# Moving a few weight-preparing steps, and one set of hash products, inside a fused attention and feed-forward kernel

## The chip, the cores and the metric

The kernel runs on one core of one Trainium2 chip. The metric is the time of one execution on the device in microseconds (us), the median of three runs. The profile is one further execution, taken by the hardware profiler; its span starts at the first instruction.

A core has five instruction streams that run side by side and wait for one another by semaphores: PE (matrix products; its weight loads are shown as PEld), DVE (vector operations), ACT (activations, copies and scalings), POOL and SP (here mostly issuers of transfers). Products are written to PSUM, and a product can only be written where an earlier one has been read out.

## The reference

Attention with hashed buckets, and a gated feed-forward block behind it:

```python
# q, k, v: (4 batches, 8 heads, 768 positions, 64); proj: (64, 6)
q_bits = einsum('bhsd,dk->bhsk', q, proj) > 0        # 6 bits make a bucket
k_bits = einsum('bhsd,dk->bhsk', k, proj) > 0
mask = q_bucket[:, :, :, None] == k_bucket[:, :, None, :]
scores = where(mask, q @ k^T / sqrt(64), -1e9)
attn = softmax(scores)
x = (attn @ v)  ->  (3072 tokens, 512)

g = x @ w_gate                                       # (512, 1536)
out = (g * sigmoid(g) * (x @ w_val)) @ w_out         # (1536, 512)
```

The three weight matrices arrive as float64 and are used as float32.

## The kernel before

Heads are taken in pairs, so there are 16 pairs: 0 to 3 are batch one, 4 to 7 batch two, and so on. Each pair has two halves of the queries (384 each), and each half has six score units, one for every 128 keys. The unit number `u` counts through them, so half h of pair n begins at `u = 12 n + 6 h`. `LATE = 48` is the start of batch two and `MOVE = 84` that of pair 7.

While batch one is attended, nothing is known yet for the feed-forward block, and the weights are made ready meanwhile: converted from float64 words in 36 pieces, and, for gate and value, combined into the sums that Strassen's scheme needs. This is written as one generator of small steps. A piece takes three VectorE operations (lines 302, 304 and 307), after ScalarE has scaled it (288, 289); a block of four pieces is followed by four forming operations (336); at the end come 12 operations on the down weights (359).

```python
    def narrow(i):
        ...
        scale_to(i + 1)
        nc.vector.tensor_single_scalar(wi, wi, 3, op=ALU.logical_shift_left)       # 302
        yield True
        nc.vector.scalar_tensor_tensor(out=wi, in0=hi, ...)                        # 304
        yield True
        nc.vector.tensor_tensor(wi, wi, lo, op=ALU.add)                            # 307
        progress["piece"] = i + 1
        load_words(i)            # asks for the next pieces, on POOL's queue
        yield True

    def prepare():
        for n in range(2 * DF // PIECE):          # six blocks
            for j in range(NJ):                   # of four pieces
                yield from narrow(n * NJ + j)
            yield from form(n)                    # four steps, then written out to DRAM
            progress["blocks"] = n + 1
        for f in range(NF):                       # twelve pieces of w_out
            yield from narrow(2 * NJ * DF // PIECE + f)
        ...                                       # twelve steps on them (359)

    def prepare_on(n):
        for _ in range(n):
            next(preparing, None)

    def scale_ahead():
        scale_to(min(progress["piece"] + 4, progress["scaled"] + 1))
```

PSUM has one tile for attend, shared in batch one with the sum of a pair's exponentials, and seven that go round for all else:

```python
    av_ps = ctx.enter_context(tc.tile_pool(name="av_ps", bufs=1, space=PSUM))
    banks = ctx.enter_context(tc.tile_pool(name="ps", bufs=7, space=PSUM))
    ...
    def total(n):
        ps = av_ps.tile([P, 512], FP32, tag="av", name="sum") if b == 0 else bank("sum")
        ...                                       # products with a column of ones (531)
        nc.vector.reciprocal(r, ps[:, 0:HQ])      # 539
        ...                                       # eight transfers by SP (544), then norm (551)
```

The next pair's hash bits come from four small products and are spread to a second set of rows by a transfer on SP's queue. Before pair 4, that queue also fetches q and k of pair 5 in eight transfers of small pieces (104).

```python
        def hash_early(todo):
            q0, q1, *ks = hash_blocks(todo)       # four products into one PSUM tile
            q0()                                  # signs of q, on ScalarE
            q1()
            spread_q()                            # SP: qb rows 64.. <- qb rows 0.. (420)
            return [...]                          # signs of k, done after the half's scores
```

The main loop takes one half after the other:

```python
    for u in range(0, N, NCH):
        n, half, _ = units[u]
        gating = u >= LATE
        ...
        for c in range(NCH):
            score(u + c)
            if u + c == 2 or not gating and half == 1 and c == NCH - 3:
                prepare_pair(1)                   # the next pair's hash products
            if c == 1 and half == 0 and 0 < n <= NP:
                total(n - 1)
            if c:
                add(u + c)
        ...
        for c in range(NCH):
            attend(u + c)
        ...
        prepare_on(0 if u == LATE else 4)
        ...
        prepare_on(0 if LATE - NCH <= u <= LATE else 3)
        if not gating:
            continue
        ...
        while atoms and (credit > 0 or not end):  # 14 up steps of the feed-forward block
            size, atom, end = atoms.pop(0)
            credit -= size
            atom()
            part += size
            ...
            if 5 < part < 14 if u == LATE else part < 9:
                prepare_on(size)
            if 6 < part < 11 or u == LATE and part > 10:
                scale_ahead()
            ...
```

From batch two on, every half carries 14 steps of the feed-forward block of the batch before: up steps (product, then copies, additions, tanh and gate on ScalarE and VectorE), or down steps. The first down product is due in the first half of pair 7, and what is then left of the preparing is done ahead of it.

Of the kernel before, what the change touches and what calls it, by code (L numbers as in the profile page):

```python
# [18 lines left out]
def kernel(  # L19
# [16 lines left out]
    NCH = S // P  # L36
# [72 lines left out]
    def load(n, names):  # L109
        if n < len(pairs):  # L110
            for name in names:
                fetch(n, name, nc.sync)
# [179 lines left out]
    def scale_ahead():  # L292
        scale_to(min(progress["piece"] + 4, progress["scaled"] + 1))
# [70 lines left out]
# [3 lines that stand above are left out]
# [102 lines left out]
    LATE = NP * 2 * NCH  # L469
# [5 lines left out]
    def score(u):  # L475
        n, half, c = units[u]
        qs = slice(half * HQ, (half + 1) * HQ)
        ks = slice(c * P, (c + 1) * P)
        sc = [bank("sc")[:, 0:HQ] for _ in range(2)]
        for x, start in ((T, True), (bits, False)):  # L480
            if u < 2 and not start:
                prepare_pair(1)
            for h in range(2):
                rows = slice(h * D, (h + 1) * D)
                nc.tensor.matmul(sc[h], x["k", n][rows, ks], x["q", n][rows, qs],  # L485
                                 start=start, stop=not start)
        for h in range(2):
            nc.scalar.activation(weights(u)[:, h, 0:HQ], sc[h], AF.Exp,  # L488
                                 scale=SCALE * (OFF / 2 if n <= NP else 1.0))

    def attend(u):
        n, half, c = units[u]
        b, pr = pairs[n]
        a = weights(u)
        if c == 0:
            av[n] = av_ps.tile([P, 512], FP32, tag="av", name="av")
        ps = av[n]
        width = AW if half == 0 else HQ
        for h in range(2):
            nc.tensor.matmul(ps[h * D : (h + 1) * D, 0:width], raws["v", n][:, h, c, :],  # L500
                             a[:, h, 0:width], start=c == 0, stop=c == NCH - 1)
        if c == NCH - 1:
            if half == 0:
                xT[b, pr] = xp.tile([P, S], FP32, tag="xT", name="xT")
                mean[n] = att.tile([P, 1], FP32, tag="e", name="e")
                nc.scalar.activation(mean[n], ps[:, HQ : HQ + 1], AF.Copy, scale=EPS)
            nc.scalar.copy(xT[b, pr][:, half * HQ : (half + 1) * HQ], ps[:, 0:HQ])

    def add(u):
        n, half, c = units[u]  # L510
        a = weights(u)
        if c == 1:
            acc[n, half] = att.tile([P, 2, HQ], FP32, tag="acc", name="acc")
            nc.vector.scalar_tensor_tensor(out=acc[n, half], in0=weights(u - 1)[:, :, 0:HQ],
                                           scalar=S * EPS / P, in1=a[:, :, 0:HQ],
                                           op0=ALU.add, op1=ALU.add)
        elif c > 1:
            nc.vector.tensor_tensor(acc[n, half], acc[n, half], a[:, :, 0:HQ], op=ALU.add)  # L518

    def total(n):  # L520

        b, pr = pairs[n]

        ps = av_ps.tile([P, 512], FP32, tag="av", name="sum") if b == 0 else bank("sum")
        t = [acc.pop((n, half)) for half in range(2)]
        for h in range(2):
            for half in range(2):
                g = (2 * h + half) * BLOCK  # L530
                nc.tensor.matmul(ps[g : g + BLOCK, 0:HQ], ones, t[half][:, h, :],  # L531
                                 start=True, stop=True)
        if b == 0:
            space = wo.rearrange("p f m -> p (f m)")
            space = space[:, n % 2 * 3 * HQ : (n % 2 + 1) * 3 * HQ].rearrange("p (x q) -> p x q", q=HQ)
            r, t = space[:, 2, :], space[:, 0:2, :]
        else:
            r, t = t[1][:, 0, :], t[0]
        nc.vector.reciprocal(r, ps[:, 0:HQ])  # L539
        for half in range(2):  # L540
            for h in range(2):
                g = (2 * h + half) * BLOCK
                for at in (h * D, h * D + BLOCK):
                    nc.sync.dma_start(t[at : at + BLOCK, half, :], r[g : g + BLOCK, :])
        waiting.append(lambda: norm(n, t))
        if pr == NP - 1:
            push_ffn(b)
# [200 lines left out]
    def prepare_pair(count):  # L748
        for _ in range(count):
            rest.extend(f for f in steps.pop(0)() or [] if f)  # L750

    def finish(todo):
        while todo:
            todo.pop(0)()
# [5 lines left out]
# [3 lines that stand above are left out]
        if u == MOVE:  # L763
            progress["late"] = True
            for t in late_ring:
                nc.gpsimd.memset(t[:, :, HQ:AW], 1.0)
        for c in range(NCH):
            score(u + c)
            if u + c == 2 or not gating and half == 1 and c == NCH - 3:
                prepare_pair(1)  # L770
            if c == 1 and half == 0 and 0 < n <= NP:
                total(n - 1)
            if c:
                add(u + c)
        if n <= NP:
            finish(waiting)
            finish(rest)
        if not gating and half == 0:
            steps = front(n + 1)
        if not gating and half == 0 and u > 0:  # L780
            prepare_pair(2)
        for _ in range(1 if u else 2):
# [5 lines that stand above are left out]
        if half == 1:  # L788
            load(n + 2, "qkv" if gating else "v")
        elif not gating:  # L790
            prepare_pair(2 if u > 0 else 4)
            load(n + 2, "qk")
        finish(first)
        prepare_on(0 if u == LATE else 4)
        chores = []
        if half == 1 and n >= NP:
            total(n)
            if n + 1 < len(pairs):
                chores = [None] + steps.pop(0)()
        prepare_on(0 if LATE - NCH <= u <= LATE else 3)  # L800
        if not gating:
            continue
        if n + 1 < len(pairs) and half == 0:
            steps = front(n + 1)
            chores = [None, steps.pop(0), None, steps.pop(0)]

        credit += 14 if n < 2 * NP else 15.75
        end = True
        part = 0
        while atoms and (credit > 0 or not end):  # L810
# [4 lines that stand above are left out]
            if part >= 11 or u + NCH == N and part >= 6:  # L815
                finish(waiting)
                if u + NCH == N:
                    finish([first.pop(0) for _ in range(min(2, len(first)))])
            if 5 < part < 14 if u == LATE else part < 9:
                prepare_on(size)  # L820
            if 6 < part < 11 or u == LATE and part > 10:
                scale_ahead()
            for _ in range(size):
                if chores:
                    step = chores.pop(0)
                    chores.extend(step and step() or [])
        while chores:
            step = chores.pop(0)
            chores.extend(step and step() or [])
# [34 lines left out]
```

## Time and profile before

| | |
|---|---|
| time, median of three runs | 1001.18 us (1000.87 to 1002.05) |
| span of the profiled execution | 1000.3 us |
| VectorE and ScalarE busy over the whole span | 57% and 40% |
| the same in the first 300 us | 82% and 61% |
| one preparing step on VectorE | 0.4 to 0.7 us |
| reciprocal of a sum | 2.55 us |
| six score units on PE, without a break | 5.05 us |
| attend of one half | 4.0 us |
| 14 up steps | 18.26 us |

The kernel has four batches of the same attention work, but batch one also has the preparing and no feed-forward work beside it, and batch two still has preparing steps between its up steps. The shares of the whole span are therefore averages over stages with different limits, and the change lies in the first 280 us only. In the profile, a line of the timeline gives start, duration, engine, line of the kernel, operation, output and inputs; what is in square brackets is the idle time of the engine just before, and what ended it.

### The profile page before, as it was taken

The numbers are of one execution on the slowest core, as the hardware profiler recorded it, in microseconds if no ns is written. First come the engines' busy times: TensorE is split into PE (matmuls) and PEld (weight loads), VectorE is DVE, ScalarE is ACT, GpSimd is POOL, SyncE is SP. The second block draws the span as 40 slices with busy tenths as digits, with TensorE's granted clock in tenths as the row PEclk, the third lists the DMA queues.
The fourth block names the chain that finished last, engine by engine and source line by source line (L and its number), as shares of the span: only waits on it lengthen the run. The fifth ranks groups of instructions, "written<-read, shape, count | busy, mean of one in ns | idle before, by whom it ended". The sixth has DMA issues, their size and how long they took to land.

```text
span 1000.3 us, 12465 instructions
## 1 busy us (share of the span) xinstructions
PE 990.2 (99%) x4597; PEld 599.8 (60%) x4597; DVE 570.7 (57%) x892; ACT 398.4 (40%) x885; POOL 101.5 (10%) x200
## 2 busy tenths in 40 slices
PE   9999999999999999999999999999999999999998
PEld 4444455555576765555557775555556786555687
DVE  5888998887873624556564443554556442435431
ACT  6988555465323214444342223334343211222200
POOL 3222022221000000000000000000000000111000
PEclk9999999999999999999999999999999999999999
DMA  7777595885213032333331204333122012323001
GB/s 230 214 252 244 146 259 161 216 291 148 76 43 76 22 96 84 87 100 95 97 103 34 69 17 116 92 90 100 44 84 77 22 38 64 105 82 111 29 27 37
DMA packets 120749, 106.95 MB, mean 107 GB/s; under 512 B 89264, under 2 KB 104080, under 8 KB 120688
## 3 DMA queue, kind: packets, MB, share of 16 engines
q0 software_dynamic: 19104, 73.28, 22.9%
q1 hardware_dynamic: 100784, 32.67, 14.3%
q8 instruction: 36, 0.59, 0.3%
q10 hardware_dynamic: 800, 0.20, 0.1%
q14 instruction: 25, 0.20, 0.1%
HBM read 81.79 MB, written 17.30 MB: 99 GB/s over the span
## 4 chain that ended last, share of the span: by engine, by line
PE 87%; DMA 2%; DVE 1%; SPq 1%; ACT 1%; issue 1%; POOL 0%; DVEq 0%; POOLq 0%
PE up L575 43%; PE po L575 22%; PE sc L485 12%; PE av L500 9%; PE sum L531 1%; DMA words<-in_moe_w_out_dram 1%; PE hps L403 1%; SPq L104 1%; DMA wo<-wo 1%; DMA qb<-qb 0%; DMA room<-ram 0%; DVE room L359 0%; ACT A L488 0%; DVE wo L539 0%; DVE acc L518 0%
## 5 line engine op out<-in xcount | busy, mean ns | idle before, releaser
L575 PE MATMUL up<-xT,room 128*128 128x384 f32 x768 | 260.9, 488 | 0.0
L575 PEld LDWEIGHTS up<-xT,room 128*128 128x128 f32 x768 | 144.6, 190 | 106.7 <-issue 9.8
L575 PE MATMUL up<-xc,room 128*128 128x384 f32 x576 | 197.4, 486 | 0.0
L485 PE MATMUL sc<-qT,kT 64*128 64x384 f32 x768 | 161.5, 494 | 0.2 <-DVE c L562 0.2
L575 PEld LDWEIGHTS up<-xc,room 128*128 128x128 f32 x576 | 109.5, 190 | 76.3
L579 DVE TENSOR_TENSOR c<-c,up 128x384 f32<-128x384 f32 x72 | 39.8, 553 | 180.1 <-PE up L575 179.7
L518 DVE TENSOR_TENSOR acc<-acc,A 128x768 f32<-128x768 f32 x128 | 122.7, 958 | 14.4 <-ACT A L488 1.0
L318 POOL DMA_DIRECT2D room<-ram x96 | 52.4, 546 | 714.3 <-PE up L575 707.2
L488 ACT ACTIVATE A<-sc 128x384 f32<-128x384 f32 x256 | 105.6, 499 | 3.5 <-PE sc L485 3.4
L485 PEld LDWEIGHTS sc<-qT,kT 64*128 64x128 f32 x768 | 67.8, 186 | 55.5 <-issue 45.7
L710 ACT COPY o<-po 128x256 f32<-128x256 f32 x48 | 17.9, 372 | 200.5 <-PE po L575 200.5
L561 ACT ACTIVATE th<-c 128x384 f32<-128x384 f32 x72 | 37.6, 522 | 128.7 <-DVE c L562 89.2
L500 PE MATMUL av<-A,vraw 128*64 128x384 f32 (+1 forms) x512 | 88.2, 486 | 0.0
L579 DVE TENSOR_TENSOR o<-o,po 128x256 f32<-128x256 f32 x36 | 15.2, 421 | 111.6 <-PE po L575 82.5
L485 PE MATMUL sc<-qb,kb 64*128 64x384 bf16 x384 | 65.4, 323 | 1.7 <-DMA qb<-qb 1.2
L488 ACT ACTIVATE room<-sc 128x384 f32<-128x384 f32 x128 | 54.0, 495 | 32.6 <-PE sc L485 32.6
L575 PE MATMUL po<-wo,hid 128*128 128x256 f32 x288 | 66.9, 382 | 0.0
L575 PE MATMUL po<-wo,room 128*128 128x256 f32 x288 | 66.3, 379 | 0.1
L575 PE MATMUL po<-room,hid 128*128 128x256 f32 x288 | 66.1, 379 | 0.0
L500 PEld LDWEIGHTS av<-A,vraw 128*64 128x64 f32 x512 | 36.7, 137 | 46.0 <-issue 44.1
L638 ACT COPY c<-up 128x384 f32<-128x384 f32 x72 | 34.4, 478 | 69.1 <-PE up L575 69.1
L575 PEld LDWEIGHTS po<-wo,hid 128*128 128x128 f32 x288 | 54.1, 190 | 12.1 <-issue 4.9
(110 smaller groups left out, 969.4 us busy)
## 6 DMA issues: line engine op xcount, KB each, us to landing
room<-ram POOLq DMA_DIRECT2D x48, 512.0 KB, 4.8
room<-ram POOLq DMA_DIRECT2D x48, 384.0 KB, 3.9
vraw<-in_v_dram SPq DMA_DIRECT2D x16, 384.0 KB, 3.3
ram<-room POOLq DMA_DIRECT2D x12, 512.0 KB, 4.8
out_dram<-o SPq DMA_DIRECT2D x48, 128.0 KB, 1.7
room<-in_moe_w_out_dram POOLq DMA_DIRECT2D x10, 512.0 KB, 6.3
qraw<-in_q_dram SPq DMA_DIRECT2D x48, 96.0 KB, 3.2
hid<-in_moe_w_gate_dram POOLq DMA_DIRECT2D x9, 512.0 KB, 6.9
```

The lines of the kernel that those rows point to most:

```text
L104: queue.dma_start(blocks[at : at + BLOCK], src[b, 2 * pr + h][:, x * BLOCK : (x + 1) * BLOCK].rearrange("(a p c) d -> p c a d", c=NCH, p=B ...
L318: nc.gpsimd.dma_start(places[k % 2][:, PARTS[go], :], ram[k % NG][:, PARTS[go], :])
L403: nc.tensor.matmul(tile_[i * BLOCK : (i + 1) * BLOCK, 0:HQ], hash_w, T[name, n][:, half * HQ : (half + 1) * HQ], start=True, stop=True)
L485: nc.tensor.matmul(sc[h], x["k", n][rows, ks], x["q", n][rows, qs], start=start, stop=not start)
L488: nc.scalar.activation(weights(u)[:, h, 0:HQ], sc[h], AF.Exp, scale=SCALE * (OFF / 2 if n <= NP else 1.0))
L500: nc.tensor.matmul(ps[h * D : (h + 1) * D, 0:width], raws["v", n][:, h, c, :], a[:, h, 0:width], start=c == 0, stop=c == NCH - 1)
L518: nc.vector.tensor_tensor(acc[n, half], acc[n, half], a[:, :, 0:HQ], op=ALU.add)
L561: nc.scalar.activation(th, g, AF.Tanh, scale=0.5)
L575: nc.tensor.matmul(ps, a, x, start=start and i == 0, stop=i == len(pairs_) - 1, skip_group_check=True)
L579: nc.vector.tensor_tensor(o, a, b, op=op)
L638: nc.scalar.copy(tile_of(g, spot), c)
L710: nc.scalar.copy(o, c)
```

## The change

Three conditions are changed. The second halves of batch one's pairs 0 to 2 call two preparing steps fewer. From unit 66 on, which is the second half of pair 5, the halves that have up steps call preparing steps behind ten of these and no longer behind eight. And the next pair's hash products are put behind the third score unit of the half before it, not behind the fourth. The purpose is to relieve VectorE in batch one, where it has the sums of the exponentials, the reciprocals and the preparing to do at once, and to have the hash bits earlier; no operation is added or taken out.

```diff
         for c in range(NCH):
             score(u + c)
-            if u + c == 2 or not gating and half == 1 and c == NCH - 3:
+            if u + c == 2 or not gating and half == 1 and c == 2:
                 prepare_pair(1)
@@
-        prepare_on(0 if LATE - NCH <= u <= LATE else 3)
+        prepare_on(0 if LATE - NCH <= u <= LATE else 3 if gating or not half else 1)
         if not gating:
             continue
@@
-            if 5 < part < 14 if u == LATE else part < 9:
+            if 5 < part < 14 if u == LATE else part < (9 if u < LATE + 3 * NCH else 11):
                 prepare_on(size)
```

## The prediction

> **What bounds the kernel now.** I read the page first: part 1 for the shares, part 2 for where they are not even, then the chain that ended last, the waits of PE, stretches cut at the scores of each half pair, and the order of DVE, ACT, SP and PE around each break.
>
> ```profile
> PE 990.2 (99%) x4597; PEld 599.8 (60%) x4597; DVE 570.7 (57%) x892; ACT 398.4 (40%) x885; POOL 101.5 (10%) x200
> ```
>
> PE bounds the span, so only a moment in which PE stands or crawls can be gained. The stretches (us, then busy us of PE, PEld, DVE, ACT, POOL) show where these lie in batch one, pairs 2 to 4, one stretch from the first scores of a half to those of the next:
>
> ```profile
> 53.45:67.63 14.18, 12.46 (x82) 5.83 (x80) 13.32 (x16) 10.25 (x25) 4.80 (x8) 1.00 0.94 344
> 67.63:77.68 10.05, 10.05 (x69) 4.42 (x68) 7.42 (x12) 9.92 (x22) 0.58 (x1) 1.00 0.58 154
> 77.68:92.12 14.44, 12.65 (x83) 5.84 (x81) 13.68 (x16) 10.34 (x25) 3.71 (x7) 1.00 0.85 292
> 102.17:113.79 11.62, 10.45 (x71) 4.53 (x69) 10.92 (x13) 8.04 (x18) 0.53 (x1) 1.00 0.70 215
> ```
>
> A first half without a break would take 5.05 (scores) + 0.78 (sum) + 4.04 (attend), all from the chain, + twice 0.8 (transposes): about 11.5. Pairs 2 and 3 lose 2.7 and 2.9 us there. What PE waited for, and the order on DVE and PE:
>
> ```profile
> PE av L500 <- DVE wo L539: 3.0, 2, 1.7
> PE sc L485 <- DMA qb<-qb: 1.2, 1, 1.2
> ```
> ```profile
> 58.75 0.69 DVE L304 SCALAR_TENSOR_TENSOR room<-hid,room 128x512 int32<-128x512 int32 x1
> 59.57 0.69 DVE L307 CUSTOM_DVE_ANT_0 room<-hid,room 128x1024 uint16<-128x1024 uint16 x1
> 60.18 2.55 DVE L539 RECIPROCAL wo<-sum 128x384 f32<-128x384 f32 x1
> ...
> 84.67 2.55 DVE L539 RECIPROCAL wo<-sum 128x384 f32<-128x384 f32 x1
> ```
> ```profile
> 62.79 1.52 PE L500 MATMUL av<-room,vraw 128*64 128x386 f32 x8 [1.67 <-DVE wo L539]
> ...
> 80.81 0.85 PE L531 MATMUL sum<-acc,ones 128*32 128x384 f32 x6 [0.35 <-DVE acc L518]
> ...
> 87.27 1.52 PE L500 MATMUL av<-room,vraw 128*64 128x386 f32 x8 [1.38 <-DVE wo L539]
> ```
>
> The sum and attend share one PSUM tile, so attend waits for the reciprocal that reads the sum. The reciprocal stands on DVE right behind the preparing steps of the second half before it: the sum ended by 56.9, the reciprocal began at 60.18.
>
> Later, in batch two, PE is dense, but two score stages are longer than 5.05: 216.82 to 222.94 (6.12) and 245.24 to 251.28 (6.04). There ACT stands behind a weight that has not landed, tanh comes late, and DVE frees a bank late:
>
> ```profile
> 216.18 0.67 ACT L288 ACTIVATE wo<-words 128x512 f32<-128x512 f32 x1 [1.77 <-DMA words<-in_moe_w_out_dram]
> ...
> 244.45 0.67 ACT L288 ACTIVATE wo<-room 128x512 f32<-128x512 f32 x1 [2.79 <-DMA room<-in_moe_w_out_dram]
> ```
> ```profile
> 246.11 0.56 DVE L562 SCALAR_TENSOR_TENSOR c<-th,c 128x384 f32<-128x384 f32 x1 [2.32 <-ACT th L561]
> ...
> 266.06 0.56 DVE L579 TENSOR_TENSOR c<-c,up 128x384 f32<-128x384 f32 x1 [2.01 <-PE up L575]
> ...
> 276.42 0.55 DVE L562 SCALAR_TENSOR_TENSOR c<-c,up 128x384 f32<-128x384 f32 x1
> ```
>
> From 266.06 to 292 DVE has no idle gap, and the second down product begins behind it (chain: DVE to 288.24, PE from 288.29).
>
> [...] a ready reciprocal stands 3.3 us behind steps that nobody is waiting for. [...] the kernel uses seven in rotation and one for attend, and the trace shows scores waiting for a bank that DVE's last gate holds. [...] the 48 KB spread of q's bits lands after 4.77 us behind eight small-piece fetches, against a median of 1.9.
>
> **The change part by part.** (1) Fewer steps. A block has 4 x 3 narrowing and 4 forming steps, about 0.61 us each (seven took 55.90 to 60.18). The second halves of pairs 0, 1, 2 call 5 instead of 7; pair 3's had 4 and keeps them. By the start of batch two 47 steps are done, not 53.
>
> Pair 0's cut lets the first reciprocal start when its sum ends, near 34.45 instead of 35.67; PE did not wait there. The normalising and all behind it shift by about 1.2, less 0.3 because other kinds of steps fall into the next half: pair 1's sums are ready by about 55.15, not 55.93. The sum products then take 0.8 instead of 1.4: -0.6. Then five steps (302, 304, 307, 302, 304: 2.95) instead of seven (4.28): the reciprocal ends near 60.65 instead of 62.73. PE is ready for attend at 60.45: it starts at 60.7 instead of 62.79, **-2.1** in all.
> In pair 3 the sum still waits, since its sums come through normalising and its transfers, which shift with the reciprocal (18 us from reciprocal to sum, 16.8 on PE). Five steps again (a forming one, 302, 304, 307, 302: 2.94) instead of seven (4.08): **-1.1** on the second wait. Together **-3.2** by about 91 us.
>
> (2) The hash products move one unit (0.8 us) earlier. The spread before pair 4 does not move for it:
>
> ```profile
> 92.46 2.75 SPq L104 DMA_DIRECT2D qraw<-in_q_dram  x4
> 95.25 3.83 SPq L104 DMA_DIRECT2D kraw<-in_k_dram  x4
> 99.59 0.55 SPq L420 DMA_DIRECT2D qb<-qb  x1
> ```
>
> q's signs end at 97.85 on ACT, and SP gets to the spread at 99.59, behind eight fetches. So the 1.2 us wait for qb stays, whole. In the other pairs it was ready anyway. The price: the products' bank now comes round for the first score of the next half, not its second unit, and the signs of k that read it end there within 0.2 us of PE (53.56 against 53.45). **+0.1**.
>
> (3) The six steps come back in the three halves from 188 us on, two each, behind up steps nine and ten. Counts after each half of batch two: before 61, 76, 91, 106, 121, 136; after 55, 70, 85, 102, 119, 136. No product has to pull a block forward (block 5 of the weights is due at 65 calls with 69 done, the ninth at 97 with 99).
> - First half with two more (188 on): DVE has 1.77 + 0.27 of idle there for 1.3 us of steps. The weight ACT scales last is again one that was asked for three up steps before: **+0.2**.
> - Second (217 on): the fourth scaling after the sixth step now takes a piece whose load is issued one up step later (1.3 us), behind another 512 KB. It lands about 1.0 later, and tanh, gate and bank with it: **+1.0**.
> - Third (245 on): two steps more in the stretch where DVE has no gap, 2 x 0.61: **+1.2**, at the scores or at the down product, not at both.
>
> Sum: -3.2 + 0.1 + 0.2 + 1.0 + 1.2 = -0.7; with a little slack in the later terms I take -0.9: 1001.18 - 0.9 = 1000.3.
>
> **The rivals.** The late steps are absorbed: DVE is idle for 2.3 us waiting for tanh in the second half, and if that gap moves to the third, and the load lands no later, nearly all of -3.2 stays: 998.1. Against it: DVE's gapless 22 us before the down product.
> The later loads collide: the forming of the last block and its 1.8 MB now fall at 203 to 209, beside the fetch of the next weights, and the piece asked for at 208.7 comes 2 us later than I think; then scores at 217 lose as much: 1002.3. For it: that fetch took 7.5 us already. Against it: before, 2 MB moved in the same microseconds.
> The hash move is the gain: if SP's last fetch at 95.25 (3.83 us for four, against 2.75) waited for something that comes earlier now, the qb wait of 1.2 could go: another -0.8. Nothing in the waits of SP says so.
>
> **Range and chances.** The gain is sure to about 0.4, the cost lies between 0.3 and 3.5. 80%: 998.5 to 1001.9. All of it is under 0.4% of the time; 2% would be 20 us, more than all waits of PE.
>
> **What would show it.** Right: attend of pair 2 starts near 60.7 and of pair 3 near 84.1, with gaps under 0.5; the sum of pair 3 still breaks off; the qb wait is still 1.2 at about 101; the up stage starts near 110.6 instead of 113.79; then PE gives back about 1 us near 245 and 1.2 between 272 and 288. Wrong: an up stage that starts later than 112, or a lead of 3 us that is still there at 300, or one that is gone at 220.

## Result, and the profile after

The changed kernel takes **1007.11 us**, the median of four runs (1006.69 to 1008.13); the kernel before takes 1001.62 beside it (1000.87 to 1002.75). The ratio is **1.0055**, 95% interval 1.0038 to 1.0073. Predicted were 1000.3 and a range of 998.5 to 1001.9: the change makes the kernel slower, by some 5.5 us, and the range missed it. The profiled executions differ by 4.4 us (spans 1004.7 and 1000.3).

The page of the changed kernel, part 1, in the same order of engines as before:

```profile
PE 993.3 (99%) x4597; PEld 601.0 (60%) x4597; DVE 570.0 (57%) x892; ACT 399.9 (40%) x885; POOL 101.2 (10%) x200
```

PE is busy 3.1 us longer with the same 4597 products (993.3 against 990.2): part of it ran at a lower clock (0.80 on average from 100.44 to 117.76). The stretches, cut as before at the first scores of each half (pair 2's halves, pair 3's first half, and pair 4's first half; us, then busy us of PE, PEld, DVE, ACT, POOL, granted clock, share of the DMA engines, GB/s), show where:

```profile
53.44:66.61 13.17, 12.61 (x82) 5.79 (x80) 12.44 (x14) 10.34 (x25) 3.41 (x7) 1.00 0.93 319
66.61:76.68 10.07, 10.07 (x71) 4.44 (x70) 6.89 (x11) 9.48 (x21) 2.95 (x4) 1.00 0.59 147
76.68:90.40 13.72, 12.57 (x84) 5.82 (x82) 12.92 (x15) 10.11 (x24) 3.23 (x6) 1.00 0.58 184
...
100.44:117.76 17.32, 13.33 (x70) 5.46 (x68) 16.12 (x19) 9.05 (x19) 3.50 (x6) 0.80 0.61 164
```

Pair 2's first half is 1.0 us shorter than before (13.17 against 14.18) and pair 3's 0.7 (13.72 against 14.44). Pair 4's first half, which had 11.62, has 17.32, with a mean clock of 0.80. It begins 1.7 us earlier than before, at 100.44 instead of 102.17, and its up stage starts 4.0 us later, at 117.76 instead of 113.72. From there on the delay hardly changes: 4.1 at 216.8 of the kernel before, 3.5 at 245.2, 4.2 at the first down product (288.27 against 284.03). So nearly all of the loss in this execution arises within one half pair.

PE's waits (us in total, times, longest), and its order of work around them:

```profile
PE sc L485 <- DMA qb<-qb: 4.0, 1, 4.0
...
PE sum L531 <- DVE acc L518: 1.3, 2, 1.0
...
PE av L500 <- DVE wo L539: 0.2, 1, 0.2
```
```profile
61.77 1.52 PE L500 MATMUL av<-room,vraw 128*64 128x386 f32 x8 [0.24 <-DVE wo L539]
...
80.35 0.85 PE L531 MATMUL sum<-acc,ones 128*32 128x384 f32 x6 [1.04 <-DVE acc L518]
...
105.50 0.47 PE L485 MATMUL sc<-qb,kb 64*128 64x384 bf16 x1 [3.99 <-DMA qb<-qb]
```

The wait of attend for the reciprocal, 3.0 us in two places before, is gone but for 0.2. In its place the wait for q's bits before pair 4 has grown from 1.2 to 4.0. VectorE and SP in the stretch before it, first two lines of the kernel before, then the changed one:

```profile
93.74 1.02 DVE L551 SCALAR_TENSOR_TENSOR xT<-xT,e,wo 128x768 f32<-128x768 f32 x1 [1.46 <-DMA wo<-wo]
```
```profile
87.24 5.04 SPq L544 DMA_DIRECT2D wo<-wo  x8
```
```profile
82.94 2.55 DVE L539 RECIPROCAL wo<-sum 128x384 f32<-128x384 f32 x1
...
97.03 1.02 DVE L551 SCALAR_TENSOR_TENSOR xT<-xT,e,wo 128x768 f32<-128x768 f32 x1 [6.48 <-DMA qraw<-in_q_dram]
```
```profile
85.52 6.80 SPq L544 DMA_DIRECT2D wo<-wo  x8
92.42 3.91 SPq L104 DMA_DIRECT2D qraw<-in_q_dram  x4
96.36 3.94 SPq L104 DMA_DIRECT2D kraw<-in_k_dram  x4
100.83 0.55 SPq L420 DMA_DIRECT2D qb<-qb  x1
```

The reciprocal comes 1.7 us earlier than before (82.94 against 84.67), but normalising comes 3.3 us later: at 97.03, against 93.74 before, where VectorE had been idle for 1.46 us instead of 6.48. SP's issues are slower as well (6.80 us for the eight transfers `wo<-wo`, against 5.04): the spread is issued at 100.83 instead of 99.59.

### The profile page after: what moved, and what is told of

It is laid out like the page before. It is cut to its first block, busy times and chain, and to the rows that moved or that the text cites. A ratio compares the mean times of both kernels' runs of the same rounds, so it can differ in the third digit from the quotient of the medians.

```text
span 1004.7 us, 12470 instructions
## 1 busy us (share of the span) xinstructions
PE 993.3 (99%) x4597; PEld 601.0 (60%) x4597; DVE 570.0 (57%) x892; ACT 399.9 (40%) x885; POOL 101.2 (10%) x200
## 4 chain that ended last, share of the span: by engine, by line
PE 74%; issue 2%; DVE 1%; DMA 1%; ACT 0%; POOL 0%; POOLq 0%; DVEq 0%
PE up L575 34%; PE po L575 21%; PE sc L485 9%; PE av L500 7%; PE sum L531 1%; DMA room<-in_moe_w_out_dram 1%; PE hps L403 1%; DVE room L359 0%; DVE acc L518 0%; ACT A L488 0%; DVE wo L359 0%; DVE c L562 0%; POOL room L318 0%; ACT wo L288 0%; ACT room L289 0%
## 5 line engine op out<-in xcount | busy, mean ns | idle before, releaser
L485 PE MATMUL sc<-qT,kT 64*128 64x384 f32 x768 | 163.7, 500 | 0.2 <-DVE c L562 0.2
```

## What moved in front of SP's transfers

The steps that were cut also trigger transfers. Behind a block's fourth forming step its sums are written out, in two transfers of 512 KB; for blocks 0 and 1 a set is also loaded back (`bring`), behind the write that it reads; and a narrowed piece asks for the next. The cuts in pairs 0 and 1, four steps together, move the end of block 1 from the first to the second half of pair 2. POOL's issues, of the kernel before and then of the changed one:

```profile
74.14 0.58 POOL L339 DMA_DIRECT2D ram<-room  x1 [10.63 <-DVE room L336]
78.26 1.09 POOL L318 DMA_DIRECT2D room<-ram  x2 [3.55 <-issue]
```
```profile
81.19 0.58 POOL L339 DMA_DIRECT2D ram<-room  x1 [4.83 <-DVE room L336]
84.66 1.09 POOL L318 DMA_DIRECT2D room<-ram  x2 [2.89 <-issue]
85.74 0.54 POOL L339 DMA_DIRECT2D ram<-room  x1
86.27 0.53 POOL L273 DMA_DIRECT2D words<-in_moe_w_val_dram  x1
86.78 0.53 POOL L273 DMA_DIRECT2D hid<-in_moe_w_val_dram  x1
```

The load of block 1's set (512 and 384 KB), a write of sums and two pieces of 512 KB now start at 84.7 to 87.3 us, together with the eight small transfers of the reciprocal (85.52 on). Two stretches of six microseconds, before and after, same columns as above:

```profile
84.00:90.00 6.00, 4.62 (x34) 2.34 (x32) 5.79 (x6) 3.88 (x9) 0.53 (x1) 1.00 1.02 413
90.00:96.00 6.00, 6.00 (x48) 2.92 (x44) 4.30 (x6) 4.55 (x13) 0.00 (x0) 1.00 0.59 123
```
```profile
84.00:90.00 6.00, 5.89 (x40) 2.77 (x37) 5.58 (x6) 3.71 (x10) 2.65 (x5) 1.00 0.66 189
90.00:96.00 6.00, 6.00 (x47) 3.01 (x47) 0.55 (x1) 5.51 (x14) 0.00 (x0) 1.00 1.09 319
```

Before, most of the bulk (413 GB/s) is over when the eight transfers (from 87.24 on) and the fetch of q and k need the engines (123 GB/s, 59% busy). After, it is the other way round: the engines are full from 90 to 96, and VectorE works 0.55 us of the six. The transfers issued from 84 to 108 us (count, KB each, median us from issue to landing), before and then after:

```profile
wo<-wo SPq DMA_DIRECT2D x8, 48.0 KB, 3.6
qraw<-in_q_dram SPq DMA_DIRECT2D x4, 96.0 KB, 3.0
```
```profile
wo<-wo SPq DMA_DIRECT2D x8, 48.0 KB, 6.0
qraw<-in_q_dram SPq DMA_DIRECT2D x4, 96.0 KB, 4.5
```

That is a correlation between two executions. The experiments below ask whether it is the cause.

## The experiments

Every ratio is to the kernel before, run on the same chip; brackets hold the 95% interval. Lines of code are those of the changed kernel unless it says otherwise. In one table, with the start of the first up stage of the profiled execution (113.7 before, 117.8 changed):

| run | time, us | ratio | up stage starts |
|---|---|---|---|
| e1: cut steps, hash products back | 1007.54 | 1.0051 [1.0038, 1.0064] | 116.6 |
| e2: hash products alone | 1002.21 | 0.9997 [0.9988, 1.0006] | 112.6 |
| e3: changed, pair 5's q and k later | 1007.74 | 1.0049 [1.0035, 1.0063] | 117.8 |
| e4: changed, PE kept busy in the wait | 1007.61 | 1.0059 [1.0041, 1.0078] | 117.0 |
| e5: cut in pairs 1 and 2 only | 1013.17 | 1.0099 [1.0079, 1.0119] | 111.9 |
| e6: e5 and e3 together | 1011.42 | 1.0097 [1.0081, 1.0112] | 111.8 |
| e7: before, pair 5's q and k later | 1006.09 | 1.0039 [1.0026, 1.0053] | 113.5 |
| e8: before, with bulk added | 1005.94 | 1.0045 [1.0031, 1.0059] | 117.4 |
| e9: e5, look-ahead 3 | 1000.02 | 0.9974 [0.9964, 0.9983] | 112.2 |
| e10: before, look-ahead 3 | 1000.62 | 0.9988 [0.9982, 0.9995] | 113.4 |
| e11: changed, look-ahead 3 | 1005.41 | 1.0030 [1.0019, 1.0041] | 116.2 |
| e12: changed, nothing made up | 1011.00 | 1.0084 [1.0070, 1.0098] | 117.4 |
| e13: changed, block 1's load later | 1005.68 | 1.0035 [1.0020, 1.0049] | 115.1 |
| e14: e13, look-ahead 3 | 1003.83 | 1.0014 [1.0005, 1.0023] | 115.0 |

**Which part does it: e1 and e2.** e1 keeps the cut and the making-up and puts the hash products back; e2 does the reverse on the kernel before.

```diff
-            if u + c == 2 or not gating and half == 1 and c == 2:
+            if u + c == 2 or not gating and half == 1 and c == NCH - 3:
```

> The changed kernel with the hash products back behind the fourth score unit; the steps stay as changed. Traffic theory (the cut of steps moves block 1's forming and loads from 74-85 us to 81-93 us, onto SP's transfers for pair 3's sum and pair 5's q and k, so the spread before pair 4 is issued and lands late, PE stands 4 us and then runs at half clock for 6 us): as slow as the changed kernel, 1006 to 1008, with the wait for qb still near 4 us. Hash theory (the earlier products crowd ScalarE and PE and the spread suffers from it): back near 1001 or lower, wait for qb near 1.

> The kernel before with only the hash products moved behind the third score unit; all preparing steps as before. Traffic theory: 1001 to 1002, the wait for qb stays between 0.8 and 1.5 us, since the spread stands behind SP's fetches. Hash theory: 1005 to 1008.

e1 loses as much as the whole change, e2 nothing: the moved steps carry all of it, and what the hash products cost or bring is too small to see (under 1 us). In e2's profile the wait for q's bits is gone, against what was expected, and the up stage starts 1.1 us earlier than before, yet the median of the time is the same. In e1 VectorE again idles 6.1 us before normalising (97.07). Its wait for q's bits is only 2.5 us, but waits for sums (1.1) and for the reciprocal (0.85) follow it in pair 4: the delay is split in another way.

**Two waits side by side: e3 and e4.** e3 takes the fetch of pair 5's q and k out of SP's way: it goes behind pair 4's first half, where v is fetched. e4 leaves the waits and puts 16 small products that nobody reads ahead of the waiting one, so that PE doesn't stand.

```diff
-            load(n + 2, "qkv" if gating else "v")
+            load(n + 2, "qkv" if n >= NP - 1 else "v")
@@
-            load(n + 2, "qk")
+            load(n + 2 if n < NP - 1 else len(pairs), "qk")
```
```diff
+            if u == LATE and not start:
+                fill = bank("fill")
+                for _ in range(16):
+                    nc.tensor.matmul(fill, sides["k", 1][:, 0:P], sides["k", 1][:, 0:512],
+                                     start=True, stop=True)
```

> The changed kernel, but pair 5's q and k are fetched after the second half of pair 3 has been attended and not after its first half: the spread no longer stands behind these eight fetches. Traffic theory: the wait for qb goes (under 0.3 us) and with it the half clock: 1007.1 - 4.0 - 2.9 = about 1000, and lower if the bulk transfers around 90 us are done by then. Hash theory: 1005 or more, for the place of the products is unchanged. It could lose some of it again if the fetches, now near 100 us, delay the transfers for pair 3's normalising and with them the up stage.

> The changed kernel with 16 bf16 products of 512 columns, whose result nobody reads, put ahead of the product that waits for qb: about 3.4 us of work in the 4 us gap. If the half clock comes from PE's standing still: granted clock 1.0 from 101 to 114 us and 1007.1 - 2.9 = about 1004.2, with the qb wait itself unchanged (what is idle shrinks to under 1 us, the product still starts near 105.5). If the half clock has another cause (the stage or the load of the chip): clock 0.5 again after 104 us and 1007 or a little more.

Both are misses. In e3 the spread is issued at 95.20, and the wait for it is gone. The up stage starts at 117.8 all the same, because another wait takes its place; first VectorE, then PE's longest wait in e3:

```profile
96.48 1.02 DVE L551 SCALAR_TENSOR_TENSOR xT<-xT,e,wo 128x768 f32<-128x768 f32 x1 [5.85 <-DMA wo<-wo]
```
```profile
106.86 1.50 PE L531 MATMUL sum<-acc,ones 128*32 128x384 f32 x6 [3.69 <-DVE acc L518]
```

Normalising is late with no fetch of q and k ahead of it, so the fetch isn't what holds it up, although the profile of the changed kernel names q's fetch beside it. And pair 3's second sums, which VectorE makes behind normalising, come about as late as the spread (in the changed kernel they end at 107.3, and PE has the spread bits at 105.5). In e4 the clock stays at 1.0 from 102 to 112 us, and the up stage still starts only 0.8 us earlier: waits for sums and reciprocal (0.7 and 0.85) show up instead. The halved clock had cost PE some 3 us in the changed kernel (3.1 of busy time), but most of that lay beside VectorE's delay.

**Cutting elsewhere: e5 and e6.** Here pair 0 keeps its two steps, and only pairs 1 and 2 are cut; block 1 then ends in pair 2's first half, as in the kernel before. e6 adds e3's move.

```diff
-        prepare_on(0 if LATE - NCH <= u <= LATE else 3 if gating or not half else 1)
+        prepare_on(0 if LATE - NCH <= u <= LATE else 3 if gating or not half or n == 0 else 1)
```

> The changed kernel, but pair 0's second half keeps its seven steps: four steps fewer before batch two and not six, and block 1 of the weights is formed, written and loaded in the first half of pair 2 as in the kernel before (near 74 to 80 us). Traffic theory: pair 2's normalising no longer waits 6 us (it comes near 92 to 93 us), PE's waits before pair 4 are 1.5 us or less and the up stage starts near 111 to 112; the time is 999 to 1002, depending on what the later halves give back. Rival (too few steps are done before batch two, wherever their transfers lie): 1004 or more.

> As the kernel with four steps fewer, and pair 5's q and k fetched after pair 3's second half. If SP's order is what is left of the wait before pair 4: 1 us lower than that kernel, 998 to 1001, and the wait for qb gone. If the transfers for the normalising set the pace there anyway: the same as that kernel.

In batch one, e5 is what the prediction had hoped for: block 1's load is issued at 79.58, normalising comes at 92.64 (idle 2.2), the wait for q's bits is 1.0, and the up stage starts at 111.9, 5.9 us earlier than in the changed kernel and 1.8 earlier than before. Yet the time is the longest of all, 1013.17 (its profile is of the shortest of its six runs, 1008.04). It loses in batch two, where PE waits 2.2, 1.75 and 0.84 us at three score stages for banks that VectorE's gate holds (L562), behind ScalarE:

```profile
187.82 0.67 ACT L288 ACTIVATE wo<-room 128x512 f32<-128x512 f32 x1 [4.19 <-DMA room<-in_moe_w_out_dram]
...
219.22 0.67 ACT L288 ACTIVATE wo<-room 128x512 f32<-128x512 f32 x1 [2.56 <-DMA room<-in_moe_w_out_dram]
```

By counting, the last piece that ScalarE scales in the halves from `u` = 60, 66 and 72 was asked for three, two and one up steps earlier in e5; in the changed kernel three, three and two. In e5 ScalarE stood 4.19 us at a weight still on its way (187.82 above) and did the tanh only behind it, at 188.95; VectorE's gate, at 189.49, had waited 4.50 us for that tanh. e6 gains no more in batch one: its wait for q's bits is replaced by 1.25 for sums and 0.6 for the reciprocal, as e3 would have it; its time, 1011.42, misses as well.

**The suspect alone, added: e7 and e8.** Both change the kernel before. e7 moves the fetch of q and k as in e3. e8 leaves every step where it is and loads the sets of blocks 0 and 1 once more, four transfers with 1.8 MB in all, ahead of the eight small transfers of pair 2's reciprocal (from 82.72 us on; the changed kernel loads 0.9 MB from 84.66 on, with a write and two pieces behind):

```diff
+        if u == 6 * NCH:
+            for x in range(2):
+                for go in range(2):
+                    bring(x, go)
```

> The kernel before with only that fetch moved: the wait for qb (1.2 us) goes, 1000 to 1001. If it comes back as a wait for the sum or for the reciprocal, or at the scores of batch two: 1001.5 to 1002.5.

> The kernel before, with the first two sets of block sums (1.8 MB) loaded a second time, from about 85.5 us on: nothing else is changed, and no step moves. Traffic theory: the eight transfers behind pair 2's reciprocal land 3 to 4 us later, its normalising comes at 96 to 98 us and not at 93.7, PE waits 2.5 us or more before pair 4's scores or sum, and the time is 1003.5 to 1006. Rival (what is slow in the changed kernel is the order of the steps on VectorE, not the transfers): 1001 to 1002.5.

e7 is slower, against what was expected: the wait for q's bits goes, but the fetch now runs beside the transfers of the last sum, and PE stands 2.1 us in the up stage for the last normalising (117.94). So moving the fetch gains nothing in the kernel before either. e8, with its VectorE steps untouched, becomes the changed kernel in batch one; its VectorE, and its two stretches:

```profile
97.78 1.02 DVE L551 SCALAR_TENSOR_TENSOR xT<-xT,e,wo 128x768 f32<-128x768 f32 x1 [6.48 <-DMA qraw<-in_q_dram]
```
```profile
84.00:90.00 6.00, 4.64 (x32) 2.27 (x30) 5.69 (x5) 2.93 (x7) 1.49 (x3) 1.00 1.04 425
90.00:96.00 6.00, 6.00 (x46) 2.97 (x44) 1.21 (x2) 5.52 (x15) 0.00 (x0) 1.00 1.03 327
```

The same 6.48 us of idle VectorE, a wait of 3.4 us for q's bits, an up stage from 117.35. Bulk at this place is enough to produce the loss of batch one.

**The suspect alone, taken away: e13 and e14.** e13 is the changed kernel, with its steps where they are and one difference: the load of block 1's set, 0.9 MB, waits until the start of batch two, where it still stands ahead of the first up steps. e14 shortens ScalarE's look-ahead on top.

```diff
                 for go in range(2):
-                    bring(i, go)
+                    if i == 0:
+                        bring(i, go)
@@
+        if u == LATE:
+            bring(1, 0)
+            bring(1, 1)
         if n <= NP:
```

> Theory (bulk transfers that now fall behind pair 2's second half hold up the small ones of SP): block 1's share of them, the load of one set of the gate and value weights, two transfers of 0.9 MB together, leaves 84 to 86 us and is asked for at the start of batch two, the steps on VectorE staying where the change puts them. About 0.9 of some 3 MB are gone from 81 to 88 us, so the normalising of pair 3 comes at 94.5 to 96 instead of 97.0, its idle time before it falls from 6.5 to 3 to 5, and the up stage starts 1 to 3 earlier than 117.8. Time 1003.5 to 1006.5. Rival 1 (the steps themselves, in their new order on VectorE, make normalising late): normalising stays at 97 and the time at 1007. Rival 2 (the load only moves the collision on, to the spread at 101): normalising earlier, but the wait for qb before pair 4 stays at 3 or more, and the time at 1006.5 to 1008.

> The same with the look-ahead of ScalarE shortened from four to three pieces. Theory (two independent losses): the shorter look-ahead takes about 2 off, as it did for the changed kernel alone, so 1001.5 to 1004.5, and the late score stages are 5.05 where they were 5.5 to 6.1. Rival (the loss in batch one and the late one are one and the same): less than 1 us between the two.

VectorE, SP and POOL of e13 (whose line numbers behind 341 are one higher), and its small transfers issued from 84 to 108 us:

```profile
91.99 1.02 DVE L552 SCALAR_TENSOR_TENSOR xT<-xT,e,wo 128x768 f32<-128x768 f32 x1 [1.40 <-DMA wo<-wo]
```
```profile
85.55 4.99 SPq L545 DMA_DIRECT2D wo<-wo  x8
90.64 2.75 SPq L104 DMA_DIRECT2D qraw<-in_q_dram  x4
93.43 3.53 SPq L104 DMA_DIRECT2D kraw<-in_k_dram  x4
97.48 0.55 SPq L421 DMA_DIRECT2D qb<-qb  x1
```
```profile
81.16 1.12 POOL L339 DMA_DIRECT2D ram<-room  x2 [4.82 <-DVE room L336]
82.28 0.53 POOL L273 DMA_DIRECT2D words<-in_moe_w_val_dram  x1
83.22 0.53 POOL L273 DMA_DIRECT2D hid<-in_moe_w_val_dram  x1 [0.41 <-ACT A L489]
```
```profile
wo<-wo SPq DMA_DIRECT2D x8, 48.0 KB, 3.3
...
qb<-qb SPq DMA_DIRECT2D x1, 48.0 KB, 6.6
```

More has changed place than the 0.9 MB. In the changed kernel POOL issued the load at 84.66, after 2.89 us without an issue, and the second write of sums and the two pieces, 0.5 MB each, right behind it; without the load these are issued 3.6 to 4.0 us earlier. With all this bulk out of the way, the eight small transfers land after 3.3 us again, and normalising comes at 91.99, 5.0 us earlier than in the changed kernel and 1.75 earlier than before: the shift that the prediction had counted on. Of the second rival a part is true: the spread, although issued 3.4 us earlier than in the changed kernel, lands after 6.6 us, perhaps because two weight pieces of 512 KB are asked for at 94.88 and 96.67, just ahead of it. They too have been moved by the cut (83.17 and 84.96 before). So PE still waits 2.6 us for q's bits, runs at half clock for 3.4 us, and starts the up stage at 115.1: 2.7 us of the 4.0 are back. The time falls by less, 1.4 us, and by medians of different chips (ratios 1.0055 and 1.0035, whose intervals overlap), so that the gain in time is less sure than the one in the trace; in e13's profile a wait of 1.1 us at 249.9 takes some of it.

**The loss in batch two: e9, e10, e11, e14.** One digit, in four kernels: ScalarE may scale three pieces ahead of VectorE and no longer four.

```diff
-        scale_to(min(progress["piece"] + 4, progress["scaled"] + 1))
+        scale_to(min(progress["piece"] + 3, progress["scaled"] + 1))
```

> The kernel with four steps fewer (pair 0 uncut), and ScalarE allowed to scale three pieces ahead of VectorE instead of four, so that it never stands behind a piece that was asked for one to three up steps before. Look-ahead theory (the later losses, 2.2, 1.75 and 0.84 us at the scores at 186, 218 and 250 us of that kernel, come from ScalarE standing behind such a piece): those three waits go, the up stage still starts near 112, and the time is 998.5 to 1001.5, some of the gain being lost where VectorE now has to wait for a scaling. Rival (the later losses come from VectorE having too many steps left): 1007 or more, as without it.

> The kernel before with only the look-ahead set to three. Look-ahead theory: the scores at 216.8 and 245.2 us take near 5.05 us instead of 6.1 and 6.0, and the time is 999.5 to 1001. Rival: no change, or slower, 1002 to 1004, because VectorE waits for scalings that are no longer ahead.

> The changed kernel with the look-ahead set to three. Its loss before batch two's up stage (4 us at 117.8) stays, its later loss goes: 1004.5 to 1006.5. If the later loss is VectorE's: 1007 or more.

In the kernel before, the two score stages of 6.1 and 6.0 us (from 216.82 and 245.24) come down to 5.05 each, and the time by 1.2 us. With e5's cut it is worth 13 us by medians of different chips, and PE no longer waits for VectorE's gate; **e9 is faster than both kernels, 1000.02 us, ratio 0.9974**. So e5 did not lose because too few steps were done before batch two, the rival whose number had come true: e9 has the same steps. Beside e10 (1000.62, on the same chip) the cut itself brings only 0.6 us, and the intervals touch. PE's waits in e9:

```profile
PE av L500 <- DVE wo L539: 1.1, 2, 0.6
PE sum L531 <- DVE acc L518: 0.6, 2, 0.4
...
PE sc L485 <- DMA qb<-qb: 0.4, 1, 0.4
```

In the changed kernel it takes off 1.7 us and leaves the loss in batch one (wait for q's bits 3.2, normalising at 96.65); from e13 to e14 it takes off 1.85. By medians the later load alone takes off 1.4, the shorter look-ahead alone 1.7, both together 3.3: they add up, as far as the noise lets one see, so the two losses are separate in these kernels. It isn't a full cure where the steps lie differently: in e11 and e14 one piece still holds ScalarE up, for 2.7 and 3.2 us at about 218.

**Is the making-up needed: e12.** The changed kernel with the six steps not made up behind the up steps, but only where they are forced ahead of the down product:

```diff
-            if 5 < part < 14 if u == LATE else part < (9 if u < LATE + 3 * NCH else 11):
+            if 5 < part < 14 if u == LATE else part < 9:
```

> The changed kernel without the third part: the halves from unit 66 on call preparing steps behind eight up steps, as before, so six steps are left over to the first down product, where they are done in one go. Up to 200 us as the changed kernel (up stage at 117.8). Six steps of 0.61 us in front of the down product: 3.7 us more there, less the 1.2 that the two extra steps cost there in the changed kernel: 1008 to 1010. If PE hides them: 1006 to 1007.5.

In e12 the last piece of the down weights, by the counts of steps, still lies as raw words where pair 7's exponentials are written, so it computes with other numbers than the weights; the operations and their order are those of the schedule. Its longest wait of PE:

```profile
PE po L575 <- DVE room L579: 3.7, 1, 3.7
```

It loses 3.9 us against the changed kernel by medians of different chips (2.9 by the ratios), in the down product. Once the steps are cut, they have to be made up.

## Why the prediction was wrong

**"The normalising and all behind it shift by about 1.2" and "its transfers, which shift with the reciprocal"** (part 1) is the first step that failed. The reciprocals did shift, but the normalising behind them did not: for pair 0's sums it came at 45.68 against 45.66, with the reciprocal 1.3 us earlier; for pair 1's at 69.71 against 70.04, with the reciprocal 1.0 earlier; for pair 2's at 97.03 against 93.74, with the reciprocal 1.7 earlier. Between the two lie eight small transfers, and I treated the 9 to 10 us from the start of one to the other as a constant, though I had read off that the spread lands after 4.77 us behind eight fetches, against a median of 1.9; they became 10.5 to 14. What stretched them for the first two pairs was not tested. The first term fell with it: pair 1's sums were complete at 56.4 us, not at 55.15 as forecast, against 56.0 before. So the queue on VectorE was relieved as worked out (two steps fewer, attend's wait 1.67 to 0.24 and 1.38 to nothing), but PE got 1.0 us of 2.1 by pair 2's attend (61.77) and 1.7 of 3.2 by pair 3's (85.55).

**"So the 1.2 us wait for qb stays, whole"** (part 2) is the step that decided the sign. It was argued for the hash move alone (in e2's profile the wait is even gone) and then used for the whole change. The count of steps beside it asked only whether a product would have to pull a block forward; it didn't ask which transfers the counted steps issue, and beside what. The wait became 4.0 us, with 2.9 us lost to the halved clock behind it, against a lead of 1.7: -1.7 + 2.8 (the wait, 4.0 less 1.2) + 2.9 (the rest, which is what the clock left over) = +4.0 at the up stage. That bulk at this place causes it is shown by adding it to the kernel before (e8) and by taking it away from the changed kernel (e13).

**Hash products, "+0.1"**: too small to be tested; e2 differs from the kernel before by less than 1 us.

**The late terms, "+0.2", "+1.0" and "+1.2"**: the mechanism, ScalarE behind a piece asked for shortly before, is real (a stand of 4.19 us in e5; with one piece less ahead, e9 gains 13 us on e5 and e10 1.2 on the kernel before, by medians). Their sizes are not explained. In the profile of the changed kernel, its shortest execution, PE lost only 0.2 us more between the up stage and the first down product than before, not 2.4: the three score stages took 5.56, 6.14 and 5.66 us, against 6.12, 5.97 and 5.08. In e1, e3 and e4, whose late steps are the same, it was 2.7, 1.8 and 2.1. Their up stages start anywhere from 116.6 to 117.8, and the score stage from about 220 us ends at 226.4 to 226.6, as in the changed kernel; but the next one ends at 255.9 to 256.5, and there at 254.9. When PE arrives doesn't decide it alone, since e3 and the changed kernel start the up stage together. In e5 it was 8.0.

**The rivals** had a collision in them, but at 203 to 209 us; the rival in which the hash move is the gain had its effect on the wait in e2's profile, where that for q's bits is gone, but no gain in e2's median. The prediction did name "an up stage that starts later than 112" as what would show it wrong, and that is where it showed. The range was too narrow because it priced the steps and not what they set off.

**What stays open.** By medians the loss is 5.5 us, and the profiles explain 4.4; the late terms, larger in e1, e3 and e4 than in the changed kernel's shortest execution, may be the rest. e5's median is 5 us above the execution that was profiled; those 5 us are in no trace. Why the fetch of k before pair 4 takes 2.78 us in e2's profile and 3.83 in the nearly identical kernel before isn't known; in e2 no wait for q's bits was left, and the time was the same. The two pieces that may hold up the spread in e13 were not moved away.

## What to carry to other kernels

A step that is moved takes its transfers with it: list what every moved step issues, and where that lands relative to the small transfers that the next dependent work waits for. Where two chains come late for the same reason (here the spread and the sums), taking one away shows nothing, so take the cause away and not a wait. Keep a look-ahead from reaching a weight that was only just asked for: in e5 ScalarE stood 4.19 us at one that was asked for three up steps before, with the tanh behind it; one piece less was worth 1.2 us in the kernel before, and the best cut of steps perhaps 0.6 on top.

## What the runs showed of the hardware

PE's clock in the changed kernel, microsecond by microsecond around its wait (columns as above; the clock is the third figure from the right):

```profile
104.00:105.00 1.00, 0.00 (x0) 0.00 (x0) 0.90 (x2) 0.00 (x0) 0.00 (x0) 0.94 1.05 183
...
106.00:107.00 1.00, 1.00 (x5) 0.36 (x3) 0.90 (x2) 0.49 (x1) 0.00 (x0) 0.50 0.78 312
...
112.00:113.00 1.00, 1.00 (x12) 0.64 (x10) 1.00 (x2) 0.79 (x2) 0.00 (x0) 1.00 0.61 184
```

Summed over such microseconds, PE was at half clock for 6.84 us after a stand of 4.0 us (the changed kernel) and for 6.82 after one of 3.7 (e3), but for 3.42 after stands of 3.4 (e8) and 2.6 (e13), and not at all after 2.5 (e1). In these runs the length was thus none, one or two times 3.4 us. How many isn't set by the stand alone: 3.34 us brought two (6.82, e12), 3.37 only one (3.42, e8). What sets it was not shown. The eight products of a sum took 1.51 us at a clock of 0.50 (107.50 in the changed kernel), against 0.85 at 1.00 (105.47 in the kernel before). By an estimate from the lengths, at half the work a microsecond, 3.42 us at half clock cost PE up to 1.7 us of work and 6.84 up to 3.4; in the changed kernel PE was busy 3.1 us longer. In e4, at a clock of 1.0, only 0.8 us of that came back at the up stage, since other waits (0.7 and 0.85 us) took its place.

How much a small transfer suffers beside bulk was new to me as well: eight transfers of 48 KB landed after 3.6 us each (median) when the bulk was just ending (the kernel before), and after 6.0 to 6.6 beside it (the changed kernel and e8). SP took 6.8 us to issue the eight in the changed kernel instead of 5.0, but 5.0 in e8 too.
